# Windows of exponentials in an S4D and token-mixer kernel: where the root, the first exponents, the pieces and the parameter chain are computed

## The chip, the core and the metric

The kernel runs on one core of a Trainium2 chip. The core has a matrix engine (PE, with its weight loads PEld shown apart), a vector engine (DVE), a scalar engine for table functions (ACT), a general engine (POOL) and a queue that issues the transfers between HBM and the on-chip memory (SP). Each engine works through its own queue in order and waits at semaphores for the others. The metric is the device time of one execution in microseconds (us).

## What is computed

An adaLN-conditioned block: a modulation vector from `c`, a layer norm of the input, an S4D convolution (a long convolution whose kernel is a sum of 256 complex exponentials for each of 448 channels), a residual, a second layer norm, and a token-mixing MLP. Cut to what matters:

```python
L, D, N = 2048, 448, 256
mod = (silu(c) @ w_mod).reshape(1, 6, 1, -1)          # sa, ca, ga, sb, cb, gb
h = layernorm(x) * (1 + ca) + sa                      # (x - mean) / sqrt(var + 1e-5)
dt = exp(log_dt)
A = -exp(log_A_real) + 1j * A_imag
C = (C_real + 1j * C_imag) * dt[:, None]
P = exp((A * dt[:, None])[:, :, None] * arange(L))
K = 2 * einsum("dn,dnl->dl", C, P).real
y = irfft(rfft(h.T, 2 * L) * rfft(K, 2 * L))[:, :L].T + h * D_skip
x = x + ga * y
h = layernorm(x) * (1 + cb) + sb
x = x + gb * (w2.T @ gelu(w1.T @ layernorm(h) + b1) + b2)
```

All of it is in 32-bit floats.

## The kernel before

The first part, up to about 390 us, makes the convolution kernel and both transforms; a second part (about 397 to 447 us) multiplies the spectra of the last channels and transforms them back; the rest is the mixer's matmuls.

The first part is a loop over 56 steps, `for s in range(tail)` (L989). A step makes half of one group of 16 channels. The engines' order is written out by hand: PE, ACT, DVE and POOL run their instructions in program order, only the transfers are placed by a scheduler. In a step

- `st_kgen(s - 2)` (L644, matmuls L653) sums the products of two steps before on PE into the kernel. When a group is complete ACT copies it (L667) and DVE adds the skip term (L672);
- `st_phase(s + 1)` (L591) makes the phases of the next step on PE into two accumulators, `xe` and `xg` (matmuls L578; there are two buffers of the pair);
- `st_step(s)` (L610) takes on ACT two absolute values and four sines (L619 to L624), in place in `xe` and `xg`; POOL (L626, L627) and DVE (L628, L629, then L631, L632) multiply them by magnitudes. Between DVE's two pairs `between()` puts DVE's waiting list and a few operations of the parameter chain (`more`);
- the lists `act` and `dve` hold small operations that ACT and DVE are to do at the next flush;
- `st_s1` (L678, matmuls L691) does the first stage of the kernel's transform. Its two copies into `yk` (L697) go to DVE if it is called with `busy` true, else to ACT.

The exponentials and the sines need different tables of ACT, so the exponentials of eight steps are made together, in a window before every eighth step (`window(s)`, L931; s = 0, 8, ..., 48; "window 8" is the one before step 8). Its eight places e make one set each: `st_exponents` on PE (L580, into the same `xe` and `xg`) and `st_exp` on ACT (L585, L589). In between lie the two kernel sums of the steps before, one first-stage transform (place 5), chain operations (`WPACE`), and, in windows 8 and 16, the row transforms of the input (`u_rows`: L501 on PE, L504 on DVE). Window 8 starts with the reciprocal root of the first layer norm's variance (`u_scale`: a square root on ACT, a reciprocal on DVE, L477 to L479), after which POOL normalises the input (L488).

The parameter chain (`chain`, L350) computes, for channels 128 to 447 in three passes q = 1, 2, 3, what the exponents and phases are made of: log, arctan and exp on ACT in a window (`angle`, `logs`), everything else on DVE, a step at a time as `more(n)` asks for it. It yields "logs" until the window has run its table functions, and "end" at the end of a pass; either ends the call of `more`.

From step 33 on, pieces of the inverse transform run between the steps (`piece`, L916): first the inverse half of the piece before (`pc_inv`, L766 and L767, then a copy L772), then the forward half of the next (`pc_s2`, L750, and on DVE the products L758). In the windows of steps 40 and 48 both halves are at place 4. The column transforms of the input (`u_cols`, L533) run in steps 17 to 31.

```python
WPACE = [[0] * 8, [0, 5, 4, 4, 4, 4, 4, 4], [0, 5, 4, 4, 4, 4, 4, 4], [2] * 8]
pace = [2] * 32
```

Of the kernel before, what the change touches and what calls it, by code (L numbers as in the profile page):

```python
# [14 lines left out]
AF = mybir.ActivationFunctionType  # L15
ALU = mybir.AluOpType
# [19 lines left out]
EPS = 1e-5  # L36
# [180 lines left out]
def tile_adaln_s4d_mixer(ctx, tc, i, out):  # L217
# [20 lines left out]
    with ExitStack() as es:  # L238
# [111 lines left out]
        def chain(q):  # L350


            n = min(P, D - P * q)
            cr, ci, a, aim = (raws[q][nm][0:n] for nm in ("A_C_real", "A_C_imag", "A_log_A_real", "A_A_imag"))
            xa, ya, s, t, u, ph, p64 = (
                qp.tile([P, N], F32, tag=nm, name=nm)[0:n] for nm in ("xa", "ya", "s", "t", "u", "ph", "p64")
            )

            def split(src, places):
                hl = qp.tile([P, 2, N], F32R, tag="hl", name="hl", bufs=3)[0:n]  # L360
                V.tensor_copy(hl[:, 0], src)
                yield
                tt(hl[:, 1], src, hl[:, 0].bitcast(F32), ALU.subtract)
                for k, v in places:
                    nc.sync.dma_start(pars[q][v, k, 0:n], hl.bitcast(F32))
                yield


            S.activation(xa, cr, AF.Abs, scale=0.5)
            S.activation(ya, ci, AF.Abs, scale=0.5)  # L370
            tt(s, xa, ya, ALU.add)
            yield
            tt(ya, ya, xa, ALU.subtract)
            yield
            ts(s, s, 2.0**-120, None, ALU.max)
            yield

            ts(t, s, 2.0**-40, 2.0**80, ALU.is_lt, ALU.mult)
            yield
            ts(u, t, 1.0, None, ALU.max)  # L380
            yield
            V.reciprocal(xa, s)
            yield
            tt(s, s, u, ALU.mult)
            yield
            tt(ya, ya, xa, ALU.mult)
            yield
            tmp[q] = a, s, u, xa, ya
            while q in tmp:
                yield "logs"  # L390
            ya = u
            yield from split(a, [(0, 1), (1, 1)])
            stt(s, t, -80 * math.log(2.0) / 2.0**80, s, ALU.mult, ALU.add)
            yield
            stt(s, ya, 0.5, s, ALU.mult, ALU.add)
            yield
            ts(s, s, ldt2[0:n, q : q + 1], None, ALU.add)
            yield
            yield from split(s, [(2, 1)])
            yield "exponents"  # L400

            ts(ph, aim, dt4[0:n, q : q + 1], None, ALU.mult)
            yield
            ts(u, ph, MAGIC, MAGIC, ALU.add, ALU.subtract)
            yield
            tt(ph, ph, u, ALU.subtract)
            yield
            yield from split(ph, [(0, 0)])

            ts(u, ph, 128.0, MAGIC, ALU.mult, ALU.add)  # L410
            yield
            ts(u, u, MAGIC, None, ALU.subtract)
            yield
            stt(p64, ph, 128.0, u, ALU.mult, ALU.subtract)
            yield
            yield from split(p64, [(1, 0)])

            ts(xa, xa, i2p, -0.125, ALU.mult, ALU.add)
            yield
            ts(u, cr, 0.0, -2.0, ALU.is_lt, ALU.mult)  # L420
            yield
            stt(xa, u, 1.0, xa, ALU.add, ALU.mult)
            yield
            ts(xa, xa, 0.25, None, ALU.add)
            yield
            ts(u, ci, 0.0, -2.0, ALU.is_lt, ALU.mult)
            yield
            stt(xa, u, 1.0, xa, ALU.add, ALU.mult)
            yield
            stt(xa, ph, 63.0, xa, ALU.mult, ALU.add)  # L430
            yield
            ts(u, xa, MAGIC, MAGIC, ALU.add, ALU.subtract)
            yield
            tt(xa, xa, u, ALU.subtract)
            yield
            yield from split(xa, [(2, 0)])
        def logs():

            for q, (a, s, u, xa, ya) in tmp.items():
                S.activation(u, ya, AF.Square)  # L440
                S.activation(s, s, AF.Ln)
                S.activation(u, u, AF.Ln, bias=1.0)
                S.activation(a, a, AF.Exp, bias=ldt[0 : a.shape[0], q : q + 1])
            tmp.clear()

# [28 lines left out]
            V.bn_aggr(mv[:, r], st)  # L474

        def u_scale():
            S.activation(rs, mv[:, :, 1], AF.Sqrt, bias=eps_t)  # L477
            V.reciprocal(rs, rs)
            stt(nm, mv[:, :, 0], -1.0, rs, ALU.mult, ALU.mult)  # L479

        yts = {}
# [448 lines left out]

        def window(s):  # L931
            angle()
            if s == 8:
                u_scale()
            if s == 8:
                u_norm(0)
                u_norm(1)
            logs()
            st_exponents(s)
            for e in range(BATCH):  # L940
                st_exp(s + e)

                if e + 1 < BATCH:
                    st_exponents(s + e + 1)
                else:
                    st_phase(s)
                mellow()
                flush(dve)
                flush(act)
                if s < 32:  # L950
                    more(WPACE[s // 8][e])
                if s == 0 and e >= 4:
                    u_stats(e - 4)
                if s == 8 and e == 0:

                    tt(mod[0], mod[0], mod[2], ALU.mult)
                    tt(mod[1], mod[1], mod[2], ALU.mult)
                if e < 2 and s:
                    st_kgen(s - 2 + e)
                elif e == 5:  # L960
                    st_s1(True)

                if s in (8, 16):
                    some(u_rows, rows, (2, 2, 2, 2, 2, 0, 1, 1)[e])
                elif s == 24 and e != 5:
                    some(u_cols, cols, 1)
                if s >= 40 and e == 4:
                    piece(pieces[0] < NP)
                if s == 0 and e in (4, 5):
                    st_mag2(e - 4)  # L970
                elif s and (e < 2 or s >= 32):
                    st_mag2(s + e)
                if s == 8 and e == 0:
                    u_norm(e + 2)
                if s == 0 and e == 1:
                    x_load(4, 4, G)
                if s == 0 and e == 3:
                    for r in range(4):
                        dsk_copy(r)
            if s == 0:  # L980

                S.activation(one, one, AF.Sin)
# [6 lines left out]
        for s in range(tail):  # L989
# [33 lines left out]
            if s >= NHALF:  # L1023
                flush(dve)
                mellow()
            else:
                if s % BATCH > 1:
                    st_kgen(s - 2)
                if (s + 1) % BATCH:
                    st_phase(s + 1)  # L1030
                st_step(s, between)
            flush(act)
            if s == NHALF:
# [242 lines left out]
```

## Time and profile before

| | us |
|---|---|
| three timed runs | 755.12, 760.1, 760.35 (median 760.1) |
| profiled execution | 756.5 |
| its span, first to last instruction | 754.4 |
| steps and windows (first part) | 0 to about 390 |
| second part of the spectra | 397 to 447 |
| mixer | 447 to 754 |

A timeline row has the start and length in us, the engine, the line, the operation, output and inputs with their shape, the count of merged instructions, and in brackets the idle time before it and the instruction that ended it. PE's ends are modelled, so consecutive rows may overlap.

### The profile page before, as it was taken

The page shows a single profiled execution, that of the slowest core. Times are in us where ns is not written, and L with a number is a line of the kernel's source. Part 1 is how long each engine was busy: PE and PEld are TensorE (multiplying, and loading weights), DVE is VectorE, ACT ScalarE, POOL GpSimd, SP SyncE. Part 2 cuts the span into 40 slices and gives each one's busy share as a digit, 9 for nine tenths or more (in the row PEclk, how much of TensorE's full clock was granted, in tenths as well). Part 3 has the DMA queues.
Part 4 walks back from the last instruction along what each step waited for, and adds up shares of the span by engine and source line. Part 5 has one row for each costly group of instructions (what it writes and reads, how often), then busy time and mean ns, then how long its engine had stood idle before and what let it go on. Part 6 is the DMA issues. An engine that isn't in the chain of part 4 may idle for free. (4 is left out here: it accounts for less than half of the span.)

```text
span 754.4 us, 18189 instructions
## 1 busy us (share of the span) xinstructions
PE 667.2 (88%) x7136; PEld 494.9 (66%) x7136; DVE 446.7 (59%) x868; ACT 453.6 (60%) x850; POOL 250.6 (33%) x293
## 2 busy tenths in 40 slices
PE   1769898889979788888989966999999999999997
PEld 0444344445424556565679963777899999999996
DVE  7693879789477485674753335777652263434341
ACT  6856588878868998889854436778742242222220
POOL 6673267267256776667633310000000000000000
PEclk9988769879989989999899995999999999999999
DMA  6963423479996745464459888676566426555530
GB/s 159 250 147 95 188 87 133 187 184 221 262 250 199 200 88 161 114 171 125 114 160 265 275 245 234 192 208 186 156 164 173 129 76 191 154 173 165 166 105 34
DMA packets 106067, 128.00 MB, mean 170 GB/s; under 512 B 13691, under 2 KB 91263, under 8 KB 105855
## 3 DMA queue, kind: packets, MB, share of 16 engines
q1 hardware_dynamic: 105166, 124.23, 58.2%
q0 software_dynamic: 816, 2.62, 1.3%
q8 instruction: 56, 0.92, 0.5%
q14 instruction: 29, 0.23, 0.1%
HBM read 91.46 MB, written 34.87 MB: 167 GB/s over the span
## 5 line engine op out<-in xcount | busy, mean ns | idle before, releaser
L203 ACT CAST whi<-w 128x896 fp32r<-128x896 f32 x64 | 60.1, 941 | 145.9 <-PE o L1243 88.8
L212 DVE TENSOR_TENSOR wlo<-w,whi 128x896 fp32r<-128x896 f32 x64 | 69.4, 1088 | 81.4 <-ACT whi L203 72.1
L626 POOL TENSOR_TENSOR G<-mag,gs 128x512 f32<-128x512 f32 x56 | 72.0, 1285 | 118.0 <-ACT gs L622 118.0
L1135 PE MATMUL acc<-h3h,whi 128*128 128x448 f32 x224 | 83.3, 372 | 0.0
L1136 PE MATMUL acc<-h3l,whi 128*128 128x448 f32 x224 | 81.9, 366 | 0.1
L578 PE MATMUL xg<-tab,lph 64*128 64x512 f32 x112 | 68.8, 617 | 14.7 <-DVE E L632 11.4
L1243 PE MATMUL o<-ul,whi 128*128 128x448 f32 x224 | 81.3, 363 | 0.0
L1242 PE MATMUL o<-uh,whi 128*128 128x448 f32 x224 | 81.2, 362 | 0.0
L1137 PE MATMUL acc<-h3h,wlo 128*128 128x448 f32 x224 | 81.1, 362 | 0.0
L1244 PE MATMUL o<-uh,wlo 128*128 128x448 f32 x224 | 80.6, 360 | 0.0
L578 PE MATMUL xe<-tab,lph 64*128 64x512 f32 x112 | 67.7, 612 | 11.7 <-ACT gs L623 8.7
L653 PEld LDWEIGHTS kg<-E,G 128*32 128x32 f32 x3584 | 58.0, 117 | 27.5 <-issue 15.4
L627 POOL TENSOR_TENSOR G<-mag,gs 128x512 f32<-128x512 f32 x56 | 72.0, 1286 | 0.0
L653 PE MATMUL kg<-E,G 128*32 128x64 f32 x3584 | 67.7, 232 | 1.9 <-issue 1.4
L628 DVE TENSOR_TENSOR E<-m,xe 128x512 f32<-128x512 f32 x56 | 38.2, 682 | 49.6 <-ACT xe L621 29.6
L758 DVE TENSOR_TENSOR z<-kx,u 128x448 f32<-128x448 f32 x64 | 36.8, 617 | 46.3 <-PE kx L750 43.0
L607 POOL TENSOR_TENSOR m<-mag,w 128x512 f32<-128x512 f32 x56 | 59.2, 1058 | 4.4
L619 ACT ACTIVATE ab<-xe 128x512 f32<-128x512 f32 x56 | 33.6, 600 | 37.6 <-PE xe L578 19.8
L1135 PEld LDWEIGHTS acc<-h3h,whi 128*128 128x128 f32 x224 | 42.4, 189 | 13.1 <-ACT whi L203 8.5
L589 ACT ACTIVATE mag<-xe 128x512 f32<-128x512 f32 x56 | 35.2, 629 | 16.7 <-PE xg L578 14.0
L578 PEld LDWEIGHTS xe<-tab,lph 64*128 64x128 f32 x112 | 24.3, 217 | 30.5 <-ACT gs L623 10.5
L1242 PEld LDWEIGHTS o<-uh,whi 128*128 128x128 f32 x224 | 42.0, 188 | 3.3
(213 smaller groups left out, 1518.4 us busy)
## 6 DMA issues: line engine op xcount, KB each, us to landing
w<-in_B_w_dram SPq DMA_DIRECT2D x64, 224.0 KB
w<-in_B_w_dram SPq DMA_DIRECT2D x32, 448.0 KB
u<-us_d SPq DMA_DIRECT2D x48, 224.0 KB
yu_d<-yt SPq DMA_DIRECT2D x16, 448.0 KB
yi<-yu_d SPq DMA_DIRECT2D x16, 448.0 KB
us_d<-uo SPq DMA_DIRECT2D x16, 448.0 KB
v_d<-vt SPq DMA_DIRECT2D x32, 224.0 KB
vt<-v_d SPq DMA_DIRECT2D x32, 224.0 KB
```

The lines of the kernel that those rows point to most:

```text
L203: self.nc.scalar.copy(hi, w)
L212: eng.tensor_tensor(lo, w, hi.bitcast(F32), ALU.subtract)
L578: T.matmul(out[k], lhs[r], rhs[r], start=start, stop=stop)
L626: G.tensor_tensor(Gt[:, 1], mg_, v32(sg), ALU.mult)
L627: G.tensor_tensor(Gt[:, 0], mg_, v32(cg_), ALU.mult)
L653: T.matmul(kgs[g][32 * q : 32 * q + 32, m], Gt[:, c, d], E[:, c, d], start=h == 0 and c == 0 and m == 0, stop=h == 1 and c == 1, skip_grou ...
L1135: nc.tensor.matmul(acc[f], hi[:, fs], h3h[:, r], start=r == 0, stop=False)
L1136: nc.tensor.matmul(acc[f], hi[:, fs], h3l[:, r], start=False, stop=False)
L1137: nc.tensor.matmul(acc[f], lo[:, fs], h3h[:, r], start=False, stop=r == 15)
L1242: nc.tensor.matmul(o, hi[:, ks], uh[kh][:, k], start=kh == 0 and k == 0, stop=False)
L1243: nc.tensor.matmul(o, hi[:, ks], ul[kh][:, k], start=False, stop=False)
L1244: nc.tensor.matmul(o, lo[:, ks], uh[kh][:, k], start=False, stop=kh == 1 and k == 6)
```

## The change

It touches seven places.

1. `u_scale`: the square root and the reciprocal are replaced. ACT now computes exp(-0.5 ln(var + eps)) inside `logs`, behind the logarithms of the chain and ahead of its exponential; DVE improves the result with one Newton step (four operations) and then makes the shift as before.
2. `window`: `logs` comes ahead of `u_scale`, and the first exponents of the window are not made there, but for window 0.
3. The loop over the steps: in the last step before a window, where there are no phases to make, `st_exponents(s + 1)` is issued ahead of `st_step(s)`.
4. In the windows of steps 40 and 48 the inverse half of a piece moves to place 2; place 4 keeps the forward half.
5. The first-stage copies L697 of windows 8 and 16 go to ACT instead of DVE.
6. The chain before the logs: the reciprocal and its product come earlier, and a maximum and a product become one operation (7 yields instead of 8).
7. The chain at the end: the angle with its two signs takes five operations instead of six, so that a pass has 28 yields behind the logs instead of 29.

```diff
             ts(s, s, 2.0**-120, None, ALU.max)
             yield
+            V.reciprocal(xa, s)
+            yield
+            tt(ya, ya, xa, ALU.mult)
+            yield
             ts(t, s, 2.0**-40, 2.0**80, ALU.is_lt, ALU.mult)
             yield
-            ts(u, t, 1.0, None, ALU.max)
-            yield
-            V.reciprocal(xa, s)
-            yield
-            tt(s, s, u, ALU.mult)
-            yield
-            tt(ya, ya, xa, ALU.mult)
+            stt(s, t, 1.0, s, ALU.max, ALU.mult)
             yield
...
-            ts(xa, xa, i2p, -0.125, ALU.mult, ALU.add)
-            yield
-            ts(u, cr, 0.0, -2.0, ALU.is_lt, ALU.mult)
-            yield
-            stt(xa, u, 1.0, xa, ALU.add, ALU.mult)
-            yield
-            ts(xa, xa, 0.25, None, ALU.add)
-            yield
-            ts(u, ci, 0.0, -2.0, ALU.is_lt, ALU.mult)
-            yield
-            stt(xa, u, 1.0, xa, ALU.add, ALU.mult)
+            ts(xa, xa, 4 * i2p, -0.5, ALU.mult, ALU.add)
+            yield
+            ts(u, cr, 0.0, 0.5, ALU.is_ge, ALU.subtract)
+            yield
+            tt(xa, xa, u, ALU.mult)
+            yield
+            ts(u, ci, 0.0, 0.5, ALU.is_ge, ALU.subtract)
+            yield
+            stt(xa, xa, 0.5, u, ALU.add, ALU.mult)
             yield
...
-        def logs():
+        def logs(root=False):
-            for q, (a, s, u, xa, ya) in tmp.items():
+            for a, s, u, xa, ya in tmp.values():
                 S.activation(u, ya, AF.Square)
                 S.activation(s, s, AF.Ln)
                 S.activation(u, u, AF.Ln, bias=1.0)
+            if root:
+                S.activation(rs, mv[:, :, 1], AF.Ln, bias=eps_t)
+                S.activation(rs, rs, AF.Exp, scale=-0.5)
+            for q, (a, s, u, xa, ya) in tmp.items():
                 S.activation(a, a, AF.Exp, bias=ldt[0 : a.shape[0], q : q + 1])
             tmp.clear()
...
         def u_scale():
-            S.activation(rs, mv[:, :, 1], AF.Sqrt, bias=eps_t)
-            V.reciprocal(rs, rs)
+            tt(nm, rs, rs, ALU.mult)
+            stt(nm, mv[:, :, 1], EPS, nm, ALU.add, ALU.mult)
+            ts(nm, nm, -0.5, 1.5, ALU.mult, ALU.add)
+            tt(rs, rs, nm, ALU.mult)
             stt(nm, mv[:, :, 0], -1.0, rs, ALU.mult, ALU.mult)
...
             angle()
+            logs(s == 8)
             if s == 8:
                 u_scale()
-            if s == 8:
                 u_norm(0)
                 u_norm(1)
-            logs()
-            st_exponents(s)
+            if s == 0:
+                st_exponents(s)
             for e in range(BATCH):
                 st_exp(s + e)
...
                 elif e == 5:
-                    st_s1(True)
+                    st_s1(s > 16)
...
+                if s >= 40 and e == 2:
+                    piece(False)
                 if s >= 40 and e == 4:
                     piece(pieces[0] < NP)
...
                 if (s + 1) % BATCH:
                     st_phase(s + 1)
+                elif s + 1 < NHALF:
+                    st_exponents(s + 1)
                 st_step(s, between)
```

## Prediction of the time

> **What bounds the kernel now.** I read the profile page, then a table of engine busy time cut at the stages, then the timeline of every engine around the six stretches the change touches. In the stage table each row has the stretch, its length, the busy time of PE, PEld, DVE, ACT and POOL, the granted clock, the DMA share and GB/s. The rows are the window of exponentials before step 8, the one before step 24, the one before step 48, and the mixer's matmuls.
>
> ```profile
> PE 667.2 (88%) x7136; PEld 494.9 (66%) x7136; DVE 446.7 (59%) x868; ACT 453.6 (60%) x850; POOL 250.6 (33%) x293
> 70.20:98.00 27.80, 24.73 (x270) 9.91 (x272) 19.36 (x48) 16.72 (x30) 8.10 (x11) 0.74 0.38 144
> 189.00:208.20 19.20, 17.75 (x299) 9.19 (x299) 9.05 (x24) 16.11 (x32) 4.16 (x6) 1.00 1.01 261
> 337.00:351.00 14.00, 13.43 (x305) 9.38 (x297) 5.87 (x10) 11.59 (x23) 10.07 (x17) 1.00 0.56 150
> 467.00:754.00 287.00, 282.96 (x1391) 253.69 (x1390) 141.05 (x276) 112.66 (x188) 0.00 (x0) 0.99 0.53 153
> ```
>
> The last 287 us are matmuls without a gap and the change does not touch them; what it can win lies in the first 390 us and comes out as an earlier start of all that follows. There no engine is the bound throughout: PE, ACT and DVE hand work round in a ring, and each stretch has its own last wait. So I cost the parts stretch by stretch, against the profiled execution (756.5 us, span 754.4, 2.1 around it). The three timed runs were 755.12, 760.1 and 760.35, so their median stands 3.6 above that execution; the mean of all four is 758.0.
>
> **Window 8: the root and the copies.** Rows of the timeline (start, length, engine, line, operation; in brackets the idle time before it and what ended it):
>
> ```profile
> 70.93 1.28 ACT L477 ACT_TABLE_LOAD   x1
> 72.23 0.31 ACT L477 ACTIVATE rs<-mv,eps_t 128x16 f32<-128x16 f32 x1
> 72.57 0.25 DVE L478 RECIPROCAL rs<-rs 128x16 f32<-128x16 f32 x1 [2.14 <-ACT rs L477]
> 73.14 2.82 POOL L488 TENSOR_SCALAR xt<-xt,rs,nm 128x448 f32<-128x448 f32 x4 [2.44 <-DVE nm L479]
> 74.89 1.28 ACT L443 ACT_TABLE_LOAD   x1
> 74.99 0.98 PE L501 MATMUL pu<-xt,wu 32*64 32x448 f32 x8
> 77.23 0.49 PE L578 MATMUL xe<-tab,lex 64*128 64x512 f32 x1 [1.27 <-ACT mag L589]
> 78.14 0.98 DVE L956 TENSOR_TENSOR mod<-mod,mod 128x448 f32<-128x448 f32 x1 [5.03 <-ACT mod L464]
> 79.75 0.62 DVE L504 TENSOR_TENSOR yt<-pu,mod 128x448 f32<-128x448 f32 x1
> 84.24 1.76 PE L501 MATMUL pu<-xt,wu 32*64 32x448 f32 x4 [1.52 <-DVE yt L504]
> 93.60 1.29 DVE L697 COPY yk<-y 128x512 f32<-128x512 f32 x2 [0.34 <-PE y L691]
> 94.81 0.28 DVE L424 TENSOR_SCALAR xa<-xa 128x256 f32<-128x256 f32 x1
> 98.04 0.60 ACT L619 ACTIVATE ab<-xe 128x512 f32<-128x512 f32 x1 [2.57 <-PE xg L578]
> ```
>
> The square root costs ACT a table load, 1.28, and itself, at most 0.31. In its place come a logarithm and an exponential on the same 128x16 tile, at most 0.31 each, in tables that the window loads anyway. So ACT is ahead by 1.28 + 0.31 - 0.62 = about 1.0, and the copy of the modulation for which DVE waits until 78.14 comes 1.0 earlier. But the root itself comes later: it was ready at 72.54; now it must wait for the exponential's table, whose load began at 74.89, so it stands at about 74.9 + 1.3 - 1.0 = 75.2. DVE then needs five small dependent operations instead of two (0.2 to 0.3 apart, as the 0.25 of the reciprocal), so POOL starts to normalise at 76.3 to 76.7 instead of 73.14. Two of its four pieces (0.7 each) must be done before a pair of row transforms can end: PE's L501 slips from 74.99 to 77.0 or later, and its first result to 78.5 to 79.2. DVE, at 77.1, first does L956 and L957 (1.6) and reaches L504 at 78.7 instead of 79.75. The late root just fits under that cover: gain 0.6 to 1.0.
>
> The two copies of the convolution's first stage (1.29, and 0.34 of waiting) leave DVE for ACT, which has 2.57 free at 98.04, and the chain loses one 0.28 operation here. DVE is 2.0 us lighter; with the lead of 1.0 that makes 3.0. Whether this reaches the end depends on PE:
>
> ```profile
> 84.20:88.00 3.80, 3.76 (x14) 0.89 (x14) 3.66 (x11) 1.08 (x2) 0.00 (x0) 0.50 0.71 281
> 96.00:100.00 4.00, 4.00 (x14) 1.27 (x14) 2.09 (x6) 1.95 (x3) 0.00 (x0) 0.50 0.45 150
> ```
>
> From 84.2 to 100 PE is busy without a gap at a granted clock of 0.50, DVE nearly so; both are the bound. If PE stays at half clock, the window gains only what its start gains, 0.7; if the clock stays up, DVE's 3.0 come through. If it falls earlier, at the new hole before L501, the work that PE had from 75.97 to 84.24 (8.27, less the 1.27 and 1.52 of idle: 5.5) takes up to 1.76/0.98 as long, 9.9; from 77.0 that ends at 86.9, against 86.0 for the transform of 84.24 now: 0.9 lost. I take -0.7, bounds -3.0 and +0.9.
>
> **The chain ends a step sooner.** The 29 chain steps that a window's pace allows were just what chains 1 and 2 had left; now 28 are left, the twenty-ninth is the end mark, and the next chain starts in step 8 and step 16 rather than one step later. Its opening (two |x| on ACT, a sum and a difference on DVE, the operations of L369 to L373) stands in DVE's queue ahead of the cosine products L631 and L632, and those free the phases' buffer for which PE waits, with everything behind it in PE's queue.
>
> ```profile
> 102.86 0.67 DVE L631 TENSOR_TENSOR E<-mag,xg 128x512 f32<-128x512 f32 x1
> 104.80 0.58 PE L578 MATMUL xg<-tab,lph 64*128 64x512 f32 x1
> 107.12 0.63 ACT L619 ACTIVATE ab<-xe 128x512 f32<-128x512 f32 x1
> 158.03 0.69 DVE L631 TENSOR_TENSOR E<-mag,xg 128x512 f32<-128x512 f32 x1 [0.16 <-ACT xg L624]
> 159.42 0.76 PE L578 MATMUL xg<-tab,lph 64*128 64x512 f32 x1 [0.97 <-DVE E L632]
> 161.03 0.41 ACT L369 ACTIVATE xa<-A_C_real 64x256 f32<-64x256 f32 x1
> 161.42 3.35 PE L533 MATMUL pu<-yi,s 128*128 128x448 f32 x4
> 162.45 1.38 DVE L373 TENSOR_TENSOR ya<-ya,xa 64x256 f32<-64x256 f32 x1
> 163.75 0.67 DVE L631 TENSOR_TENSOR E<-mag,xg 128x512 f32<-128x512 f32 x1
> 167.27 0.60 ACT L619 ACTIVATE ab<-xe 128x512 f32<-128x512 f32 x1 [2.57 <-PE xe L578]
> 215.57 3.33 PE L533 MATMUL pu<-yi,s 128*128 128x448 f32 x4 [4.32 <-DMA s<-in_S_dram]
> ```
>
> In step 17 the opening took from 161.03 to 163.75, 2.7 us, and PE was then busy with L533, so nobody waited. In step 16 nothing covers it: PE waits there already (0.97, at 159.42), and behind it come L533 and the next phases, for which ACT waits at 167.27. Moved there, it makes step 19 later by up to 2.7. What can swallow it is the wait of 4.32 for a table at 215.57, where the load and not PE comes last; the DMA share of 1.01 in window 24 says that loads run at their limit, not that they would come at the same time. I take half, +1.3 (bounds 0 and +2.7). In step 8 the same 2.7 moves the end of the phase from 105.4 to 108.1, against ACT's own start at 107.12: at most +1.0; ACT's two |x| are merely swapped between steps; I take +0.4. The chain's other lost operations lie in steps where DVE is not last: nothing.
>
> **Window 16.** The two copies go to ACT here too, ahead of the last exponential; ACT then still waits 0.60 for PE's phase at 153.51 (below), so neither DVE nor the copies are last: 0. If that cover is gone, the copies, 1.1 long and free to start only when PE is done, cost the part that does not fit before it; I put +0.2 to the bounds.
>
> **First exponents ahead of the last step's rest.** PE issues the window's first exponents behind step 7, 15, ... 's kernel products instead of behind its first-stage transform, modulation and pieces.
>
> ```profile
> 153.51 0.60 ACT L619 ACTIVATE ab<-xe 128x512 f32<-128x512 f32 x1 [0.60 <-PE xg L578]
> 194.07 0.60 ACT L589 ACTIVATE mag<-xe 128x512 f32<-128x512 f32 x1 [0.17 <-PE xg L578]
> 247.57 1.16 PE L691 MATMUL y<-wc,ks 64*64 64x64 f32 x64
> 248.45 0.67 DVE L632 TENSOR_TENSOR E<-m,xg 128x512 f32<-128x512 f32 x1
> 249.22 0.47 PE L578 MATMUL xg<-tab,lex 64*128 64x512 f32 x1
> 249.75 1.10 ACT L697 COPY yk<-y 128x512 f32<-128x512 f32 x2
> 294.56 0.60 ACT L589 ACTIVATE mag<-xe 128x512 f32<-128x512 f32 x1 [0.77 <-PE xg L578]
> 339.59 0.60 ACT L589 ACTIVATE mag<-xe 128x512 f32<-128x512 f32 x1 [0.77 <-PE xg L578]
> 348.40 0.60 ACT L589 ACTIVATE mag<-xe 128x512 f32<-128x512 f32 x1 [0.69 <-PE xg L578]
> ```
>
> At windows 8 and 16 ACT did not wait for them; nothing. Window 24: 0.17 of wait goes, -0.2. Windows 40 and 48: 0.77 each goes. There the piece is also cut: its inverse half (L766, L767) moves from place 4 to place 2, so that only the forward half stands before the seventh set's exponents, whose wait of 0.69 at 348.40 it answers. But the window is PE's: 13.43 busy of 14.0, so the two cannot add up; the inverse half now delays the fifth set instead. I take -0.9 for each window (bounds 0 and -1.5).
>
> Window 32 goes the other way. The exponents' xg half must wait until DVE has read step 30's cosines (L632, to 249.12; 0.3 earlier, as the chain's last operation is gone from there). Before, the transform L691 ran in that time, 247.57 to 248.7, and the exponents at 249.22. Now L691 stands behind them, 248.8 + 0.5 + 1.1 = 250.4, and ACT's copies of it, at 249.75 before, stand ahead of the exponentials in ACT's queue: +0.7 (0 if ACT finds slack behind, +0.8).
>
> **Sum**: -0.7 + 0.4 + 1.3 + 0 - 0.2 + 0.7 - 0.9 - 0.9 = -0.3: 756.2 on the profiled execution, 757.7 on the mean of the four. I forecast 757.0, no change that can be told. All low ends give -6.2 (750.3), all high ends +5.6 (762.1).
>
> The Trainium skill's page "ScalarE: Activation LUTs", in "Table sets: the hidden batching unit", says that one set holds both ln and exp, so that exp behind ln needs no load. The row at 74.89 disagrees: a load of 1.28 stands between them. By the rule window 8 would win another 1.28, and the sum would be -1.6.
>
> **Rivals.** *The clock stays up in window 8* (0.25). The hole that now precedes the fall to 0.50 (1.52 at 84.24) shrinks, as DVE frees the buffers 1.0 earlier. Then the window is DVE's and gains 3.0, the sum is -2.6, and with step 16's cost swallowed by the later wait for the table -4.3: 753.9 to 752.2. For it speaks that DVE ran all through; against it, that the late root opens a new hole of the same size (75.97 to 77.0 and on). The Trainium skill's page "TensorE: Matmul & The Clock Gate", Part 1, has the clock rise after some 3.4 us of sustained work and asks for idle gaps under about that; by it this rival would be the rule. The trace disagrees: the clock stayed at 0.50 through the two busy rows above.
>
> *The early chain decides* (0.2). Step 16 costs the full 2.7 and step 8 1.0: the sum is +1.7, 758.2 on the profiled execution. It decides as soon as PE's wait at 159.42 grows beyond 1.0 and the table at 215.57 comes later by as much. For: PE has no gap between 159.42 and 167; against: the 4.32.
>
> *The early exponents give nothing* (0.1): in windows 40 and 48 PE is simply late one set further on. The 1.8 go, the sum is +1.5, 758.0.
>
> **Chances.** My forecast has 0.45. About 1%, 7.6 us, is what a measurement of this kernel can tell from no change. Faster than that (under 752.5) needs the clock rival with a swallowed step 16, or executions that fall as low as 755.12: 0.2. Slower (over 767.7) needs every high end and the highest level of the runs at once: 0.06. The range of 750 to 763 takes in the low ends on the profiled execution and the high ends there, with little more for the level of the runs.
>
> **What would show it.** No table load at L477's place; the first L956 near 77.1; POOL's first normalising near 76.5 and L501 not before 77. The clock between 78 and 104. The second chain's L371 in step 8, the third's in step 16, and an idle time of over 3 us before PE's xg there. In window 32, L691 behind the exponents and ACT's copies near 250.4. In windows 40 and 48 no wait between the table load and the first exponential. I am wrong if the matmul stage starts over 3 us off its 467, or if it is itself longer.

## The result and the profile after

The changed kernel took 761.21 us (median of 20 runs, 759.25 to 769.37), the kernel before beside it 758.03 (20 runs, 752.85 to 763.75): a ratio of 1.0058, 95% interval 1.0037 to 1.0080, or +4.4 us on 758. A second comparison gave 1.0028 (0.9998 to 1.0058), +2.1. A ratio leaves out the executions more than 1.5% above the fastest of their kernel. The change costs 0.3 to 0.6%, where -0.3 us was forecast. The profiled execution took 767.03 us, its span 765.3, against 756.5 and 754.4 before. That gap of 11 is more than twice what the medians and the ratios give; about 7 of it did not come again, as will be seen.

The profile's page for the kernel after, its first part:

```profile
PE 674.2 (88%) x7136; PEld 500.6 (65%) x7136; DVE 442.9 (58%) x861; ACT 454.5 (59%) x854; POOL 251.0 (33%) x293
```

DVE is 3.8 us lighter than before, as it should be. What counts is where the stretches lengthened. The table of stages of the kernel after (stretch, length, busy time of PE, PEld, DVE, ACT and POOL, granted clock, DMA share, GB/s), cut at the starts of steps 7, 8 and 11, of steps 15, 16 and 18, of steps 23 and 24, of steps 39 and 40, of steps 47 and 48, and then the mixer's matmuls. "Window 8" below is the time from the start of step 7 to that of step 8, and so for the others.

```profile
67.28:98.95 31.67, 29.39 (x342) 13.10 (x344) 20.86 (x51) 20.26 (x39) 10.81 (x12) 0.76 0.36 132
98.95:114.09 15.14, 13.04 (x164) 6.93 (x164) 11.62 (x17) 13.48 (x25) 11.34 (x12) 0.61 0.22 77
...
131.44:157.63 26.19, 24.45 (x377) 12.72 (x374) 18.33 (x45) 19.66 (x38) 6.65 (x8) 0.64 0.43 155
157.63:167.45 9.82, 3.89 (x16) 1.79 (x14) 6.38 (x11) 8.04 (x15) 6.19 (x6) 0.67 1.00 236
...
191.06:218.51 27.45, 23.91 (x369) 12.37 (x369) 13.26 (x30) 19.46 (x38) 6.06 (x7) 0.88 0.93 219
...
299.44:316.83 17.39, 15.40 (x369) 11.46 (x369) 9.26 (x17) 15.23 (x30) 12.54 (x18) 1.00 0.56 154
343.87:363.55 19.68, 17.11 (x371) 12.54 (x372) 8.83 (x17) 15.37 (x30) 12.76 (x18) 0.91 0.47 125
...
478.00:765.00 287.00, 282.81 (x1391) 253.66 (x1390) 141.02 (x276) 112.46 (x188) 0.00 (x0) 0.99 0.54 153
```

The same steps in the kernel before:

```profile
66.02:98.04 32.02, 28.95 (x342) 12.28 (x344) 21.74 (x51) 20.36 (x38) 10.11 (x12) 0.77 0.35 130
98.04:111.56 13.52, 12.94 (x168) 6.50 (x172) 9.65 (x16) 13.46 (x26) 9.80 (x10) 0.66 0.24 86
129.90:153.51 23.61, 20.49 (x378) 11.19 (x376) 18.33 (x42) 18.69 (x35) 5.66 (x7) 0.82 0.44 165
153.51:161.65 8.14, 4.40 (x17) 1.89 (x16) 6.43 (x14) 8.08 (x16) 4.50 (x5) 0.71 0.98 241
185.64:208.24 22.60, 20.68 (x369) 10.86 (x369) 12.20 (x29) 19.46 (x38) 6.20 (x7) 1.00 1.00 252
288.16:306.15 17.99, 15.55 (x369) 11.51 (x369) 9.51 (x17) 15.31 (x29) 13.20 (x19) 1.00 0.54 148
333.19:350.90 17.71, 16.22 (x369) 11.67 (x369) 9.68 (x18) 15.04 (x29) 13.19 (x19) 1.00 0.49 134
```

The mixer is the same to 0.2 us of PE's time; everything happened ahead of it. Window 8 is 0.35 shorter, steps 8 to 11 1.6 longer, window 16 2.6 longer at a granted clock of 0.64 instead of 0.82, steps 16 and 17 1.7 longer, window 40 0.6 shorter. The largest part is window 24, 4.9 longer at 0.88 instead of 1.00, and window 48 is 2.0 longer at 0.91.

Window 8 in the kernel after, timeline:

```profile
74.42 0.29 ACT L440 ACTIVATE rs<-mv,eps_t 128x16 f32<-128x16 f32 x1
74.72 1.28 ACT L441 ACT_TABLE_LOAD   x1
76.02 0.22 ACT L441 ACTIVATE rs<-rs 128x16 f32<-128x16 f32 x1
76.27 0.18 DVE L478 TENSOR_TENSOR nm<-rs 128x16 f32<-128x16 f32 x1 [4.58 <-ACT rs L441]
77.39 3.70 POOL L491 TENSOR_SCALAR xt<-xt,rs,nm 128x448 f32<-128x448 f32 x4 [5.42 <-DVE nm L482]
78.06 0.67 DVE L959 TENSOR_TENSOR mod<-mod,mod 128x448 f32<-128x448 f32 x1 [0.71 <-ACT mod L464]
78.16 0.96 PE L504 MATMUL pu<-xt,wu 32*64 32x448 f32 x2 [1.65 <-POOL xt L491]
79.75 1.00 PE L504 MATMUL pu<-xt,wu 32*64 32x448 f32 x6 [0.63 <-POOL xt L491]
80.77 1.16 DVE L507 TENSOR_TENSOR yt<-pu,mod 128x448 f32<-128x448 f32 x2 [1.49 <-PE pu L504]
```

The root stands at 76.02 + 0.22, POOL starts at 77.39, and PE has holes of 1.65 and 0.63 ahead of the row transforms; then DVE has one of 1.49. Before, PE started them at 74.99, which by this execution's later start would be 76.25. The clock, in the table of stages cut where it changes:

```profile
80.57:83.98 3.41, 3.41 (x73) 2.29 (x74) 3.14 (x6) 1.46 (x3) 3.33 (x5) 0.50 0.35 131
...
87.40:104.46 17.06, 17.06 (x174) 7.30 (x170) 11.70 (x30) 11.64 (x23) 1.95 (x2) 0.50 0.54 194
```

It falls at 80.57, right behind the holes, comes back, and falls again at 87.40 for 17 us.

Step 16 in the kernel after, timeline:

```profile
162.03 0.41 ACT L369 ACTIVATE xa<-A_C_real 64x256 f32<-64x256 f32 x1
162.78 1.18 DVE L371 TENSOR_TENSOR s<-xa,ya 64x256 f32<-64x256 f32 x1 [0.79 <-ACT ya L370]
164.00 0.42 DVE L373 TENSOR_TENSOR ya<-ya,xa 64x256 f32<-64x256 f32 x1
164.34 0.67 DVE L634 TENSOR_TENSOR E<-mag,xg 128x512 f32<-128x512 f32 x1
164.94 0.67 DVE L635 TENSOR_TENSOR E<-m,xg 128x512 f32<-128x512 f32 x1
165.71 0.76 PE L581 MATMUL xg<-tab,lph 64*128 64x512 f32 x1 [3.15 <-ACT xg L627]
167.45 0.60 ACT L622 ACTIVATE ab<-xe 128x512 f32<-128x512 f32 x1 [1.75 <-PE xe L581]
```

The chain's opening stands ahead of L634 in DVE's queue, and PE waits 3.15 for the buffer that L634 and L635 free: the bracket names an ACT row that had ended at 162.11, and PE starts 0.1 behind the end of L635.

### The profile page after: what moved, and what is told of

Its sections match the earlier page's. It is cut to its first block, busy times and chain, and to the rows that moved or that the text cites. A ratio compares the mean times of both kernels' runs of the same rounds, so it can differ in the third digit from the quotient of the medians.

```text
span 765.3 us, 18183 instructions
## 1 busy us (share of the span) xinstructions
PE 674.2 (88%) x7136; PEld 500.6 (65%) x7136; DVE 442.9 (58%) x861; ACT 454.5 (59%) x854; POOL 251.0 (33%) x293
## 5 line engine op out<-in xcount | busy, mean ns | idle before, releaser
L656 PEld LDWEIGHTS kg<-E,G 128*32 128x32 f32 x3584 | 60.7, 121 | 29.7 <-issue 20.1
L656 PE MATMUL kg<-E,G 128*32 128x64 f32 x3584 | 70.7, 238 | 3.2 <-issue 2.7
L610 POOL TENSOR_TENSOR m<-mag,w 128x512 f32<-128x512 f32 x56 | 59.6, 1065 | 4.4
L622 ACT ACTIVATE ab<-xe 128x512 f32<-128x512 f32 x56 | 33.6, 599 | 38.4 <-PE xe L581 24.2
L592 ACT ACTIVATE mag<-xe 128x512 f32<-128x512 f32 x56 | 34.8, 621 | 17.2 <-PE xg L581 12.7
L1144 PEld LDWEIGHTS acc<-h3l,whi 128*128 128x128 f32 x224 | 42.5, 190 | 3.2 <-DVE h3l L1194 0.5
L581 PEld LDWEIGHTS xg<-tab,lph 64*128 64x128 f32 x112 | 24.7, 221 | 30.2 <-ACT gs L626 9.1
```

The source lines that it names most:

```text
L581: T.matmul(out[k], lhs[r], rhs[r], start=start, stop=stop)
L656: T.matmul(kgs[g][32 * q : 32 * q + 32, m], Gt[:, c, d], E[:, c, d], start=h == 0 and c == 0 and m == 0, stop=h == 1 and c == 1, skip_grou ...
L1144: nc.tensor.matmul(acc[f], hi[:, fs], h3l[:, r], start=False, stop=False)
```

## The experiments

Two unaltered kernels come first, then versions of the changed kernel with a part undone, then the kernel before with one part alone. A "stretch" is the time from the start of one step to that of another, a step's start being ACT's first row of it (L619, after the change L622, as 98.04 and 98.95 above). Each ratio is to the kernel before, run beside it, with its 95% interval.

**The changed kernel again.** 

> The changed kernel once more, unaltered, as the level for the runs beside it. All theories: 1.006 of the kernel before (1.004 to 1.008). By the theory that the early chain costs by mechanism, step 16 starts about 4 us later than before in this profile too, and step 24 about 10; by the theory that window 24 was a mishap of one execution (its half clock and its wait for the table), step 24 stands only 5 or 6 late.

1.0028 (0.9998 to 1.0058). In its profile step 16 stood 3.3 late against the first profile of before (4.1 in the first profile of after), step 24 4.4 (10.3), step 55 4.7 (11.3). Window 24 took 22.0 and window 48 16.4. So most of the 10 at step 24 belonged to one execution, the 3 to 4 at step 16 came again.

**The kernel before again.** 

> The kernel before, unaltered, profiled a second time: the ratio is 1.000 by any theory and shows what the comparison itself scatters (0.997 to 1.003). In the first profile window 16 (start of step 15 to start of step 16) took 23.6 us, and 25.4 to 26.2 in every version of the changed kernel, whatever part was undone; window 32 14.1 against 14.8 to 18.1. If the change costs this by mechanism, both stay at 23.6 and 14.1 (within 0.5). If the first profile of before was a fortunate execution, they rise to 25 or more and 16 or more, and the 11 us that the two first profiles differ by are mostly scatter.

0.9979 (0.9938 to 1.0019). Window 16 took 22.1, again less than in the changed kernel. But window 8 took 30.24, not 32.02, and window 32 15.5: executions of the same instructions differ by that much.

**The late chain.** In the changed kernel, in `chain`:

```diff
+            yield
             tmp[q] = a, s, u, xa, ya
...
             yield from split(xa, [(2, 0)])
+            yield
```

> The changed kernel with two empty places added back to the parameter chain (one at its end, one behind its first part), so that chains 2 and 3 open in steps 9 and 17 again. Theory A, the early chain decides: steps 16 to 18 stand at most 1.5 us later than in the kernel before, step 24 at most 3, and the ratio to the kernel before falls to 1.000 (0.998 to 1.003). Theory B, the late root in window 8 and what follows from it decides: no change from 1.006. Theory C, the later place of the exponents and pieces decides: 1.003 to 1.006, with the excess at steps 32 and 48.

1.0027 (0.9993 to 1.0062), level with the changed kernel beside it. Steps 16 and 17 went back to 8.17 us (9.87), and step 24 stood 2.8 late, within Theory A's 3. But window 16 stayed at 25.7, and step 16 stood 3.2 late, where it allowed 1.5. Theory A falls as the only cause.

**The exponents back.**

```diff
-            if s == 0:
-                st_exponents(s)
+            st_exponents(s)
...
-                elif s + 1 < NHALF:
-                    st_exponents(s + 1)
```

> The changed kernel with each window's first exponents back at the window's start, none ahead of the last step's rest. By the prediction's sum the early exponents win 1.3 net (window 24 -0.2, 32 +0.7, 40 -0.9, 48 -0.9), so without them the ratio is 1.0075. By the rival that they give nothing, or only move PE's lateness, it is 1.005 or less. By the theory that they cost in windows 16 and 24 (PE's transform and copies stand behind them there), 1.002 and a step 24 that starts 4 us earlier than in the changed kernel.

1.0013 (0.9991 to 1.0035); window 16 at 26.2, window 40 at 16.8 instead of 17.4. Without the early exponents the changed kernel is not slower (1.0013 against 1.0028, within the intervals), where the prediction's sum put it at 1.0075: no gain from them shows in it.

**The copies back**: `st_s1(True)` instead of `st_s1(s > 16)`. 

> The changed kernel with the copies of the first stage's transforms back on VectorE in windows 8 and 16. By the prediction their move to ScalarE is worth part of 2.0 us in window 8 only if PE's clock stays up, and nothing in window 16: so no change, 1.006 (1.004 to 1.008), or 1.007 if VectorE is the bound there. By the theory that the copies block ScalarE's exponentials in window 16, step 16 starts at least 1.5 us earlier than in the changed kernel and the ratio is 1.003 or less.

1.0014 (0.9983 to 1.0045), over eight of twelve executions, since four at 765.61 to 767.88 fell out; window 16 at 25.4 and step 16 no earlier than in the changed kernel run beside it (156.74 against 156.81): no effect to be told, as predicted.

**The early chain alone.** In the kernel before, one empty place less at the end of `chain`:

```diff
             ts(xa, xa, 0.25, None, ALU.add)
-            yield
```

> The kernel before with a single empty place taken from the chain behind the logarithms, so that chains 2 and 3 open in steps 8 and 16; every operation is that of the kernel before. Theory A, the early chain decides: 1.003 to 1.005, steps 17 to 23 start 2 to 3 us late, and the second load of the column transforms' input (yi) stands behind a load of phase rows (lph) in the transfer queue, 3 us or more later. The prediction's price for it: +1.7 us, 1.002. If it is without effect: 1.000 (0.998 to 1.002).

1.0069 (1.0022 to 1.0115). Steps 16 and 17 took 9.84 (8.14), steps 8 to 23 93.9 (87.6). The loads stand in the other order, as in the changed kernel. Again, with more runs: 

> The kernel before with the early chain alone, once more, since its first interval was wide (1.0022 to 1.0115). Theory A: 1.004 to 1.009, steps 16 to 18 in 9.8 us against 8.1, and steps 8 to 23 in 91 or more. By the prediction's price (+1.7): 1.002. One version without the early chain also took 91 over steps 8 to 23; if that is scatter that has nothing to do with the chain, this profile may show 88 to 89, the 87 of before and the 1.7 of step 16 only.

1.0046 (1.0013 to 1.0079), 9.83 and 92.7. Taking out a single empty place costs 3.5 to 5.2 us, though the work is the same. Both intervals lie above 1; their low ends are 1.7 and 1.0 us.

**Late chain and exponents back together**, twice. 

> The changed kernel with the late chain (two empty places) and with the first exponents at each window's start: only the late root, the copies, the shorter chain and the halves of the pieces remain. If the early chain and the early exponents are the whole cost: 0.998 to 1.000, and hardly an execution above 763. If the late root in window 8 costs: 1.002 or more, with step 8 to 12 late by 2 us or more.

0.9944 (0.9886 to 1.0002); steps 8 to 23 in 88.5. This ratio rests on three of six executions (749.75, 752.91 and 759.77). The other three took 761.81, 767.58 and 770.99, though hardly one above 763 was expected if the chain and the exponents were the whole cost; with them the kernel is no faster than the one before (median 760.79 against 759.05). 

> The changed kernel with the late chain and with the first exponents at each window's start, once more, since the first interval was wide (0.9886 to 1.0002). The new root stays. By the sum of the parts taken alone (root +2.7, halves with copies -2.4): 1.000 (0.998 to 1.003), steps 8 to 23 in 87 to 88.5.

1.0002 (0.9970 to 1.0034), as the sum of the parts has it (its +2.7 for the root is a difference of the means of all executions; the ratios below give less); steps 8 to 23 in 93.8, not the 87 to 88.5 expected. The same kernel gave a short and a long stretch. The clock of the second, in the table of stages, cut where the granted clock changes:

```profile
79.43:82.84 3.41, 3.41 (x75) 2.18 (x74) 3.32 (x6) 1.46 (x3) 3.33 (x5) 0.50 0.35 134
82.84:86.25 3.41, 3.41 (x24) 0.95 (x16) 3.34 (x10) 1.68 (x4) 1.62 (x3) 1.00 0.71 260
86.25:93.08 6.83, 6.83 (x82) 3.05 (x80) 6.55 (x18) 3.95 (x8) 0.00 (x0) 0.50 0.76 284
93.08:103.32 10.24, 7.22 (x104) 3.37 (x100) 7.15 (x15) 9.67 (x18) 4.03 (x5) 1.00 0.49 177
103.32:110.15 6.83, 6.83 (x87) 3.17 (x92) 6.14 (x10) 5.86 (x12) 6.67 (x8) 0.50 0.02 7
120.39:127.21 6.82, 6.82 (x88) 3.38 (x88) 6.42 (x12) 4.57 (x10) 3.77 (x4) 0.50 0.51 192
...
140.87:157.94 17.07, 16.77 (x172) 8.32 (x172) 11.51 (x32) 10.58 (x21) 1.75 (x3) 0.50 0.53 192
```

and of the first:

```profile
80.29:104.18 23.89, 23.89 (x261) 10.41 (x259) 18.20 (x43) 14.70 (x27) 6.70 (x9) 0.50 0.53 193
...
107.60:114.42 6.82, 6.82 (x88) 2.80 (x84) 6.79 (x9) 6.01 (x13) 6.23 (x7) 0.50 0.02 5
124.66:128.07 3.41, 3.41 (x72) 2.15 (x70) 3.41 (x7) 2.93 (x6) 3.02 (x4) 0.50 0.35 124
134.90:141.73 6.83, 6.20 (x172) 4.92 (x160) 3.73 (x8) 6.77 (x13) 1.80 (x3) 0.50 0.33 115
148.55:155.38 6.83, 6.83 (x84) 4.42 (x84) 6.38 (x20) 5.60 (x12) 0.00 (x0) 0.50 0.70 254
```

Read the lengths: 3.41, 6.83 and 17.07 are one, two and five times 3.413; 23.89 is seven times. The falls too are whole multiples apart (79.43, 86.25, 103.32, 120.39, 140.87: 2, 5, 5 and 6 times). The clock is set on a grid of 3.413 us, and the grid lies elsewhere in each execution: 79.43 is 0.9 past a multiple, 80.29 is 1.8 past one. In the execution at 0.9 window 16 meets one half-clock stretch of 17 us and takes 26.2; at 1.8 it meets two of 6.8 with full clock between, and takes 22.1. That the grid's place decides this is not shown: no run sets it, and in the table below the same 1.8 stands beside 87.1, 88.5 and 91.5 us for steps 8 to 23.

**Early exponents in windows 40 and 48 only, late chain.**

```diff
-            if s == 0:
+            if s not in (40, 48):
                 st_exponents(s)
...
-                elif s + 1 < NHALF:
+                elif s + 1 in (40, 48):
                     st_exponents(s + 1)
```

> The changed kernel with the late chain, and with the first exponents ahead of the last step's rest only for windows 40 and 48. By the prediction's prices (window 8 -0.7, window 24 0, window 32 0, windows 40 and 48 -0.9 each) it beats both kernels: 0.997 of the kernel before. By the rival that early exponents only move PE's lateness it equals the version with both undone, within 0.001. Windows 40 and 48 should then not be shorter than there.

1.0006 (0.9967 to 1.0045), window 40 at 17.2 (16.5 and 17.1 with its exponents at the start). The version that by the prediction's prices should beat both kernels does not.

**The early exponents alone**, in the kernel before: parts 2 and 3 of the change, for `st_exponents` only. 

> The kernel before, with nothing changed but the place of the first exponents (ahead of the last step's rest, all windows). So far steps 8 to 23 took 86.9 to 88.5 us where neither the early chain nor the early exponents were in, and 91.5 to 93.9 with one of them or both. If the early exponents alone do it: 91 or more here, nearly all of it between steps 11 and 16, and a ratio of 1.003 to 1.006. By the prediction's prices (window 24 -0.2, 32 +0.7, 40 and 48 -0.9 each): 0.998. If window 40 is not helped by them but by the halves of the pieces: it takes 17.9 or more here, as in the kernel before.

0.9991 (0.9965 to 1.0018); steps 8 to 23 in 87.2, window 8 at 32.0, window 40 at 18.5. No gain in window 40; window 48 took 17.2 (17.7 in both profiles of the kernel before).

**The halves alone**: `if s >= 40 and e == 2: piece(False)`. 

> The kernel before, with nothing changed but the inverse half of a piece at place 2 of windows 40 and 48. If the halves are what shortens these windows: 16.6 and 16.5 us (from 17.9 and 17.7), and a ratio of 0.997 (0.994 to 1.000). By the prediction, which gave them nothing beyond the early exponents (the inverse half delays the fifth set instead): 17.9 and 17.7, 1.000.

0.9985 (0.9961 to 1.0009); window 40 17.7, window 48 17.2, where 16.6 and 16.5 were expected if the halves did it all. Up to step 40 this is the kernel before word for word, and yet steps 8 to 23 took 91.1: a long stretch without any part of the change in it.

**The root alone**: part 1, with `logs` ahead of `u_scale`. 

> The kernel before, with nothing changed but the root (logarithm, exponential and a Newton step, behind the logarithms). By the prediction window 8 (start of step 7 to start of step 8) wins 0.7 us, bounds -3.0 and +0.9: 0.999. By the profiles so far it loses: 31.7 to 32.9 with the new root, 30.2, 30.3 and 32.0 without, so 32 here and 1.001 to 1.002. Nothing is expected of it behind step 8.

1.0030 (0.9998 to 1.0062), window 8 at 31.7. Again: 

> The kernel before with the new root alone, once more (first interval 0.9998 to 1.0062). If the late root costs by taking PE's clock down at 80 instead of 84 us and keeping it there to 104: window 8 takes 31.7 to 32.1 again (30.0 to 30.3 in four of six profiles with the old root), and the ratio is 1.0015 to 1.003. By the prediction (-0.7): 0.999.

1.0017 (0.9983 to 1.0050), window 8 at 31.7.

**Halves and copies alone.** 

> The kernel before with two parts of the change, the halves of the pieces and the copies on ScalarE in windows 8 and 16. If the halves win 1.2 us in each of two windows and the copies nothing: 0.997, as with the halves alone, and faster than both kernels. If the copies free VectorE in window 8 with the early root in place: window 8 at 29.5 or less, and 0.995.

0.9970 (0.9942 to 0.9997): 756.30 against 758.77. It is the one interval of the eighteen here that lies below 1, by 0.0003; one of so many can do that by chance, and it was not run again. Window 8 took 30.26, so the copies gave nothing there.

**The changed kernel without its two suspects**: late chain, and the old square root ahead of the logarithms. 

> The changed kernel with the late chain and with the old root (square root and reciprocal ahead of the logarithms): the early exponents, the copies, the halves and the shorter forms of the chain remain. Taken alone the parts gave, in us: early chain +5.2, root +2.3, early exponents -0.7, halves -1.1, halves with copies -2.3. If these add up and the early chain and the root are the culprits: 0.996 (0.993 to 1.000), faster than both kernels. If early exponents and the other parts cost once they are together: 1.002 or more.

1.0025 (0.9994 to 1.0056): missed. Window 8 stayed at 32.0, window 16 at 25.4. Then with window 16's exponents back as well (`if s in (0, 16)` at the window's start, and `and s != 15` behind the loop's test): 

> The changed kernel with the late chain, the old root, and window 16's first exponents back at the window's start; all others stay early. Two versions with the late chain and all early exponents took 25.4 and 25.7 us for window 16, two with the late chain and none early there 22.1 and 23.0. If the early exponents of window 16 make this: 23.0 or less here, steps 8 to 23 in 87 to 88.5, and 0.997 of the kernel before. If it is scatter: any of the two values, and 1.0025 as without this edit.

1.0053 (1.0021 to 1.0084), steps 8 to 23 in 93.6, worse if anything: those exponents are not the cause of the long stretch. And early exponents with the copies in the kernel before: 

> The kernel before with the early exponents and with the copies on ScalarE in windows 8 and 16. Each alone left window 16 at 22.1. If the two together fill ScalarE ahead of the last exponentials of window 16: 25 or more there, and 1.002 or more. If they do not interact: 22 to 24, and 0.998 (the sum of the parts).

1.0021 (0.9990 to 1.0052) in time, but window 16 at 22.1 in its profile: no meeting of the two there.

All profiles side by side (us; each cell the difference of two step starts; "grid" is the first fall of the clock behind 70 us, less whole multiples of 3.413):

| kernel | grid | window 8 | 8 to 11 | 11 to 16 | 16 to 18 | 8 to 23 | window 40 |
|---|---|---|---|---|---|---|---|
| before | 1.5 | 32.0 | 13.5 | 42.0 | 8.1 | 87.6 | 18.0 |
| before again | 3.4 | 30.2 | 14.5 | 40.0 | 8.1 | 86.9 | 17.9 |
| halves alone | 2.1 | 30.0 | 14.5 | 45.0 | 8.1 | 91.1 | 17.7 |
| halves and copies | 3.4 | 30.3 | 14.5 | 40.0 | 8.1 | 87.0 | 17.5 |
| root alone | 2.6 | 31.7 | 14.2 | 40.3 | 8.2 | 87.1 | 18.2 |
| root alone again | 1.8 | 31.7 | 14.2 | 40.2 | 8.1 | 87.1 | 18.5 |
| early exponents alone | 1.9 | 32.0 | 14.5 | 40.6 | 8.1 | 87.2 | 18.5 |
| early exponents, copies | 2.0 | 32.0 | 14.5 | 40.6 | 8.1 | 87.2 | 17.9 |
| early chain alone | 2.6 | 30.3 | 15.5 | 44.6 | 9.8 | 93.9 | 18.1 |
| early chain alone again | 0.8 | 30.0 | 15.3 | 42.9 | 9.8 | 92.7 | 18.2 |
| after | 2.1 | 31.7 | 15.1 | 43.5 | 9.8 | 92.1 | 17.4 |
| after again | 2.3 | 32.0 | 15.1 | 43.1 | 9.9 | 91.9 | 17.4 |
| exponents back | 0.5 | 31.7 | 15.1 | 43.6 | 9.8 | 92.1 | 16.8 |
| copies back | 2.1 | 31.7 | 15.1 | 42.9 | 9.8 | 91.7 | 17.1 |
| late chain | 1.8 | 32.0 | 13.5 | 44.9 | 8.2 | 91.5 | 17.4 |
| both back | 1.8 | 32.1 | 14.3 | 41.2 | 8.1 | 88.5 | 16.5 |
| both back again | 0.9 | 29.7 | 14.5 | 46.3 | 8.1 | 93.8 | 17.1 |
| late chain, 40 and 48 only | 3.0 | 32.9 | 14.1 | 40.2 | 8.1 | 87.3 | 17.2 |
| late chain, old root | 3.4 | 32.0 | 13.5 | 44.4 | 8.1 | 90.9 | 17.1 |
| late chain, old root, 16 back | 0.7 | 32.0 | 14.5 | 46.0 | 8.2 | 93.6 | 17.2 |

## Why the prediction was wrong

Two terms of the sum failed: the early chain by its size, window 8 by its sign.

**The chain ends a step sooner** (+0.4 and +1.3). Its mechanism is right: in every one of the six profiles with the early chain steps 16 and 17 take 9.8 to 9.9, in every one of the fourteen without it 8.1 to 8.2. That is +1.7, within the bounds, and PE's wait of over 3 us stands where it was foretold. In steps 8 to 11 it is 15.1 to 15.5 against 13.5 to 14.5, about +1.0 by the means, the bound given there. So these two places cost 2.7 in the profiles, where the sum took 1.7: it had halved step 16's cost for a later wait that was to swallow it, and steps 18 to 23 gave back only 0.5. In time the early chain alone cost 5.2 and 3.5 us (ratios of 1.0069 and 1.0046 on 758), two to three times the sum's 1.7, with intervals that reach down to about that.

The rest lies where the sum had no term, between steps 11 and 16. Over steps 8 to 23 the profiles fall into short ones (86.9 to 88.5) and long ones (90.9 to 93.9). With the early chain all six are long, without it five of fourteen. The split is the same by the steps from 11 to 16 alone: 40.0 to 42.0 us there, or 42.9 to 46.3. The means over steps 8 to 23 are 92.4 and 89.0, 3.4 apart: 2.7 in the two places, 1.2 between steps 11 and 16, -0.5 behind. That the early chain costs is shown by the two ratios. That it also makes the stretch from 11 to 16 long more often rests on this count alone. By what it would do so is open, and it is not simply more time at half clock: over steps 8 to 23 the mean granted clock is 0.82 in the 86.9 us of the kernel before again, 0.83 in the 91.1 of the halves alone, and 0.79 in the 87.2 of the early exponents alone. The rival "the early chain decides" had the right culprit and a better price, 3.7 for the two places, but it kept the -0.7 for window 8 and so gave +1.7 in all.

**Window 8: the root** (-0.7, bounds -3.0 and +0.9). Its -0.35 in the first pair is luck, since the 32.0 before was a rare long window; by the profiles together the sign is wrong. Alone the root cost 2.3 and 1.3 us, but both intervals take in 1, so the windows have to tell it. The steps came out nearly as worked out: the window began 1.26 later than before, and less that POOL started at 76.1 (76.3 to 76.7 foretold), PE at 76.9 (77.0), L959 at 76.8 (77.1). What failed is "the late root just fits under that cover": DVE was ready and waited 1.49 for PE, PE 1.65 and 0.63 for POOL, whose pieces took 3.70 / 4 = 0.93 and not 0.7. The six profiles with the old root and the exponents at the window's start took 30.0 to 30.3 five times; the 32.0 that I worked from was the odd one. Nine of ten with the new root took 31.7 to 32.9, and the four with the old root and early exponents 32.0. Early exponents ahead of window 8, costed at nothing, go with the same length, which may be why taking out the new root alone (late chain, old root) did not bring window 8 back.

The prediction's upper bound had the clock fall early, at the new hole. The early fall by itself is not what costs: with the halves alone (old root) the clock fell at 80.64, as in the kernel after, and the window took 30.0; in "both back again" (new root) it fell at 79.43, and the window took 29.7. What goes with the length in all twenty profiles is the clock at the window's end. In the six windows of 29.7 to 30.3 it is back at 1.00 some 2.2 to 2.6 us before step 8 starts (93.08 of 95.65 in the rows above); in the fourteen of 31.7 to 32.9 it is at 0.50 when step 8 starts. Why it comes back in some and not in others no run settles. A hole is not needed for a fall either: from 82.84 to 86.25 PE was busy for all 3.41 us at 1.00, and then the clock fell.

**The copies**: nothing, as forecast. With the halves beside them window 8 stays at 30.3, and with early exponents it is 32.0 with or without them.

**Windows 40 and 48** (-0.9 each): window 40 came out at -0.6 in the first pair, window 48 at +2.0 (16.4 in the second profile of the changed kernel, -1.3). The cause was not the one given for window 40: with early exponents and no halves it takes 17.9 and 18.5; within the changed kernel they make it longer (17.1 to 17.4 against 16.5 to 17.1). It is the halves that shorten it, by 0.2 to 0.5 taken alone or with the copies. In window 48 either part alone gives 17.2 instead of 17.7. With the copies the halves come to 2.3 us by the ratio, but only about 0.8 of that stands in these two windows. The rival "the early exponents give nothing" fits the times: 0.9991 alone, and 1.0013 for the changed kernel without them, against 1.0028 with them.

**Window 24** (-0.2): the 4.9 more in the first pair came once (22.0 in the second profile). **Window 32** (+0.7): the order came as foretold, L694 at 260.25 in the kernel after behind the exponents of 258.53 and 259.85, and the window was 0.7 longer in the first pair. But the profiles scatter from 14.1 to 18.2 whatever part is in, so this proves nothing. **The clock rival** did not come: 0.76 in window 8 against 0.77.

The parts taken alone, by the mean of their ratios: chain +4.4, root +1.8, early exponents -0.7, halves and copies -2.3, together +3.2, against 4.4 and 2.1 measured; of these only the chain's and, barely, the halves' with the copies have an interval that leaves out 1. But undone from the changed kernel they do not come off one by one: late chain alone gave nothing, chain and root together nothing, chain and exponents together brought it level with before (1.0002), though the profile of that run has the long stretch (93.8). So what makes the changed kernel slower as a whole stays open beyond the two terms above.

One more thing was overlooked. The scheduler of the transfers answered the early chain by putting a load of phase rows ahead of the column transforms' input. SP's queue after:

```profile
172.42 0.30 SPq L567 DMA_DIRECT2D lph<-pars  x1
...
174.12 1.27 SPq L527 DMA_DIRECT2D yi<-yu_d  x2
```

and before:

```profile
168.91 1.27 SPq L524 DMA_DIRECT2D yi<-yu_d  x2
...
174.64 0.53 SPq L564 DMA_DIRECT2D lph<-pars  x1
```

The early chain alone has it too, the late chain does not. It seems to have cost nothing by itself: steps 18 to 23 took 23.6 us after and 24.0 before. No run puts the order back alone.

## What to carry to other kernels

Profile the kernel before at least twice ahead of pricing a change of a few us: here one window differed by 1.8 and one stretch by 4 us between executions of the same instructions. A filler operation between engines that hand work round in a ring is not free because it is short: ask which operation of the ring it is queued ahead of in each step that it can land in, and fix that place by hand. And time the parts of a bundled change alone: here the one that was priced at +1.7 cost about as much as the whole change, and two others (halves and copies) may be a gain, 0.9970 (0.9942 to 0.9997).

## What the runs showed of the hardware

The granted clock moved between 1.00 and 0.50 only, in whole multiples of 3.413 us, on a grid whose place differs from execution to execution. The Trainium skill's page "TensorE: Matmul & The Clock Gate", Part 1 ("What's actually happening"), states just that: a window of 3413 ns that runs freely and does not start with the kernel; the rows agree to 0.01. The page's other rule there, that a busy window releases the clock, the trace contradicts: PE was busy for all of the 23.89 us from 80.29 to 104.18, seven windows, at 0.50, mostly with matmuls of 32 and 64 rows. The page also puts the ramp at under 1% of a typical kernel's span and advises against fitting a cold count: the 4 us between two stretches of 87 and 91 with the same instructions, if they come from the clock, are 0.5% of this one, under its figure and yet as large as what was to be measured.

A second one: VectorE's operations took longer beside POOL's. In the kernel after the same two operations of the chain, first beside POOL's L610 and L491 (81.37 to 84.24), then with POOL idle:

```profile
81.84 0.73 DVE L361 CAST hl<-A_log_A_real 128x256 fp32r<-128x256 f32 x1
82.60 0.82 DVE L363 TENSOR_TENSOR hl<-A_log_A_real,hl 128x256 fp32r<-128x256 f32 x1
...
85.91 0.28 DVE L361 CAST hl<-s 128x256 fp32r<-128x256 f32 x1
86.22 0.42 DVE L363 TENSOR_TENSOR hl<-s,hl 128x256 fp32r<-128x256 f32 x1
```

They took 0.73 and 0.82 us beside POOL, 0.28 and 0.42 without. The other way round, POOL's first four pieces of the normalisation took 0.70 each in the kernel before, while DVE waited, and 0.93 in the kernel after, where DVE worked for part of that time.
